# Shifted exp readings as packed 64-bit additions on GpSimd, offset added by VectorE, normalisation moved to VectorE

## The chip, the core and the metric

One core of a Trainium2 chip runs the whole program. Its engines are TensorE (PE, with PEld its weight loads), VectorE (DVE), ScalarE (ACT), GpSimd (POOL) and SyncE (SP), which here only issues DMAs. The metric is the device time of one execution in microseconds; the median over the runs counts. The profile is one execution taken by the hardware profiler; its span runs from the program's first instruction to its last.

## The reference

The reference takes a 2048 x 640 input in bf16, normalises each row, and adds three things: the input, an attention block and a feed-forward block, both on the normalised rows.

```python
def _A_ref(x, wq, wk, wv, wo):            # H = 32 heads, Dh = 20, S = 2048
    q = (x @ wq).reshape(B, S, H, Dh).transpose(0, 2, 1, 3)
    k = x @ wk                            # one k and one v for all heads
    v = x @ wv
    scores = jnp.einsum("bhqd,bkd->bhqk", q, k) * (Dh ** -0.5)
    p = softmax(scores, axis=-1)
    o = jnp.einsum("bhqk,bkd->bhqd", p, v)
    return o.transpose(0, 2, 1, 3).reshape(B, S, H * Dh) @ wo
def _B_ref(x, w1, w2):                    # F = 1728
    return silu(x @ w1) @ w2
xn = layernorm(x)
return x + _A_ref(xn, ...) + _B_ref(xn, ...)
```

There is no mask. The largest part is the exponential: 32 heads x 2048 queries x 2048 keys.

## The kernel before

**Blocks.** Scores are made in transposed form: 128 keys on the partitions, 512 queries of one head along the row. One such tile is a block; it fills one bank of PSUM. There are 2048 blocks: 4 chunks of 512 queries, 32 heads, 16 key tiles. Four heads form a group; their 64 blocks are taken key tile by key tile, and 32 groups follow one another. Since a head has 20 channels only, four heads lie side by side in strips of 32 rows, and the score matmuls of three or four blocks run at the same time in four row strips of the array (line L1113). This is a *step* (`do_S`). The product of the exponentials with v (PV, L954) uses four column strips, one per head of the group, so up to four PV matmuls run together; below, such a set is called a *pass*. The other tiled matmuls (q, feed-forward, output projection; L856) also go in passes of four.

**Two ways to the exponential.** Most blocks go to ScalarE: `exp` over two or three PSUM banks at once, written as bf16 (L1147). The others go to VectorE, in integer arithmetic. The score is scaled so that adding an offset and reading the resulting 16-bit integer as the bits of a bf16 number gives a piecewise linear 2^x. One instruction per block (L1162) clamps the value to 0..32512 and writes it as int16 into a buffer `Z`. To smooth the error, each such block is read three times: as it is, with 43 added, and with 86 added to the integers; the three readings are weighted 1, 0.805 and 0.625 through three copies of v, each with a column that sums the denominator. So a block on ScalarE costs one PV matmul and a block on VectorE three. Three blocks of `Z` are collected, then `flush_z` makes the two shifted readings `Y`: the second shift (86) always on GpSimd (L1199), an int32 addition that treats two 16-bit numbers as one with a tile of the constant 65537 x shift as second input; the first shift (43) on VectorE (L1193, in its fast mode on SBUF data) or on GpSimd, whichever the planner's balance prefers. `Z` has four sets, `Y` one for each.

**The offset.** It enters before through the score matmul itself: rows of q that are otherwise padding hold the offset's two parts (`offq`, 16000 and 45), and a second copy of kT has ones in those rows. Blocks for VectorE use the second copy (`kT[:, 1]`), blocks for ScalarE the first. GpSimd makes the second copy (L1801) and, in the prologue, the offset columns and the tile `qo` from which the q buffer's padding is filled by DMA.

**End of a group.** The accumulated U (numerators and denominators) is copied from PSUM by VectorE (L1243), transposed by a DMA from SP, the reciprocals of the denominators are made on VectorE (L1227), and the product, the normalisation, is made on GpSimd (L1232), for the last group on VectorE. When a chunk's eight groups are done, SP transposes `o`, and the output projection follows. The attention's part is needed doubled, because the feed-forward carries a factor 2 and the end multiplies by 0.5; before, GpSimd doubles wo in place (L1761).

**What sets the order.** The kernel is written as operations with dependencies. A planner in the file (`Sched`, `Builder.step`) runs at build time: it gives each operation an assumed duration, simulates the five queues, and commits operations to each engine in the order that comes out. That order is then fixed in the program, and each engine works through its own queue in order, with semaphore waits between the engines. How many blocks VectorE gets, when PV runs, and where q, feed-forward and projection matmuls are put between the steps, is all decided there, by some 26 parameters that change every 32 blocks (the table `SEG`). `lock` marks GpSimd and VectorE operations that the planner keeps from overlapping. The order of each queue therefore changes as a whole when durations or parameters change.

**Libraries.** GpSimd's affine select (L1576), which makes the identity matrix, is preceded by an instruction that asks for code library 0.

Of the kernel before, what the change touches and what calls it, by code (L numbers as in the profile page):

```python
# [10 lines left out]
I16 = mybir.dt.int16  # L11
# [32 lines left out]
OFF_HI = 16000.0  # L44
OFF_LO = 45.0
# [57 lines left out]
YP_FIX = 0.15  # L103
YP_BLK = 0.426
# [81 lines left out]
class Op:  # L186
# [3 lines left out]
    def __init__(self, eng, dur, fn, deps, prio=0.0, name="", on_sched=None, mode=None):  # L190
# [21 lines left out]
        self.late = 0.0  # L212


LAT = {"pe": 0.222, "act": 0.238, "dve": 0.14, "pool": 0.19, "sp": 0.0}
INF = float("inf")


class Sched:
# [59 lines left out]
    def ready(self, op, extra=0.0):  # L279
        r = 0.0  # L280
        for d in op.deps:
# [9 lines left out]
            if a > r:  # L291
                r = a
# [181 lines left out]
class Builder:  # L474
# [748 lines left out]
    def normalise(self, g, ut, key, eng):  # L1223
# [11 lines left out]
        if eng == "pool":  # L1235
            op.lock = True
# [662 lines left out]
```

## Time and profile before

| | |
|---|---|
| time, median of 3 runs | 677.72 us (676.57 to 678.05) |
| profiled execution, span | 674.7 us; the timed runs lie 1.9 to 3.4 us above it |
| PE busy | 664.7 us, 99% |
| ACT busy | 664.3 us, 98% |
| DVE busy | 618.6 us, 92% |
| POOL busy | 558.5 us, 83% |
| mean granted TensorE clock | 1.00 in every stage |

No time beside the span is given for the profiled execution itself. Busy means that an instruction of the engine is in flight; TensorE's matmuls overlap each other and their ends are modelled, so its share tells only that it is never left alone. A group row reads: line, engine, operation, written and read tiles with shapes, count, then total busy time, mean ns of one, and idle time of the engine just before, with what ended it. Instructions on ScalarE, VectorE and GpSimd overlap a little, so a mean is longer than the distance from one to the next.

### The profile page before, as it was taken

How to read it: one execution, taken by the hardware profiler on the slowest of the kernel's cores; microseconds unless marked ns; L12 is line 12 of the kernel's file. 1: busy time of each engine (PE TensorE's matmuls, PEld its weight loads, DVE VectorE, ACT ScalarE, POOL GpSimd, SP SyncE). 2: the span in 40 equal slices, each digit the busy share in tenths (PEclk: the TensorE clock that was granted, in tenths of full speed). 3: DMA queues.
4: the chain of work that ended last, by engine and by line, in shares of the span. 5: the costliest groups of instructions: out<-in, count | busy, mean ns of one | idle time of the engine just before them, and what ended most of it. 6: DMA issues, size and time to landing. Idle time of an engine off the chain costs nothing.

```text
span 674.7 us, 22669 instructions
## 1 busy us (share of the span) xinstructions
PE 664.7 (99%) x9656; PEld 218.6 (32%) x9656; DVE 618.6 (92%) x1110; ACT 664.3 (98%) x743; POOL 558.5 (83%) x442
## 2 busy tenths in 40 slices
PE   8899999999999999999999999999999999999997
PEld 4332223333323223333323322333332332233333
DVE  7899999899999999989999999999899999999996
ACT  8999999999999999999999999999999999999995
POOL 3385889978978889997988899978989989979983
PEclk9999999999999999999999999999999999999999
DMA  7567100000014000000003210000100310001001
GB/s 208 99 235 238 46 10 8 10 18 15 14 38 106 17 10 11 10 11 18 18 9 50 57 48 10 17 2 13 25 9 19 88 51 5 18 11 28 16 9 41
DMA packets 52729, 28.05 MB, mean 42 GB/s; under 512 B 38582, under 2 KB 51990, under 8 KB 52630
## 3 DMA queue, kind: packets, MB, share of 16 engines
q1 hardware_dynamic: 51174, 26.38, 14.9%
q8 instruction: 78, 1.28, 0.8%
q10 hardware_dynamic: 1456, 0.22, 0.2%
q14 instruction: 21, 0.17, 0.1%
HBM read 11.44 MB, written 2.62 MB: 21 GB/s over the span
## 4 chain that ended last, share of the span: by engine, by line
ACT 54%; PE 41%; DVE 2%; DMA 1%; issue 0%; POOL 0%; SPq 0%
ACT sbt L1147 51%; PE psall L954 14%; PE psall L1113 13%; PE psall L856 13%; ACT sbt L1337 2%; DVE sbt L1162 1%; DMA sbt<-sbt 1%; DMA sbt<-in_A_x_dram 1%; ACT sbt L1661 0%; DVE sbt L1641 0%; POOL sbt L1199 0%; PE psall L1772 0%; DVE sbt L1193 0%; PE psall L1791 0%; DVE sbt L1243 0%
## 5 line engine op out<-in xcount | busy, mean ns | idle before, releaser
L1147 ACT ACTIVATE sbt<-psall 128x1024 bf16<-128x1024 f32 (+1 forms) x649 | 635.5, 1217 | 0.3
L1199 POOL TENSOR_TENSOR sbt<-sbt 128x768 int32<-128x768 int32 x368 | 520.5, 1443 | 79.5 <-DVE sbt L1193 54.4
L1162 DVE TENSOR_SCALAR sbt<-psall 128x512 int16<-128x512 f32 x695 | 456.6, 684 | 40.5 <-PE psall L1113 30.1
L954 PE MATMUL psall<-sbt 128*32 128x512 bf16 x3438 | 260.4, 383 | 0.1
L1113 PE MATMUL psall<-sbt 32*128 32x512 bf16 x2048 | 251.3, 384 | 3.5 <-ACT sbt L1147 1.4
L856 PE MATMUL psall<-sbt 128*32 128x320 bf16 (+2 forms) x3923 | 227.7, 331 | 0.7 <-DVE sbt L1799 0.4
L1113 PEld LDWEIGHTS psall<-sbt 32*128 32x128 bf16 x2048 | 63.1, 91 | 251.3 <-ACT sbt L1147 184.1
L856 PEld LDWEIGHTS psall<-sbt 128*32 128x32 bf16 x3923 | 81.5, 95 | 88.7 <-issue 57.8
L954 PEld LDWEIGHTS psall<-sbt 128*32 128x32 bf16 x3438 | 64.2, 95 | 96.0 <-issue 65.2
L1193 DVE TENSOR_SCALAR sbt<-sbt 128x1536 int16<-128x1536 int16 (+2 forms) x108 | 62.8, 594 | 0.1
L1337 ACT ACTIVATE sbt<-psall 128x512 bf16<-128x512 f32 x54 | 41.6, 770 | 0.0
L1342 DVE SCALAR_TENSOR_TENSOR sbt<-sbt,psall 128x512 bf16<-128x512 bf16 x54 | 36.8, 682 | 2.3 <-ACT sbt L1337 1.2
L1232 POOL TENSOR_TENSOR sbt<-sbt 128x320 bf16<-128x320 bf16 x31 | 22.6, 728 | 6.4 <-DVE sbt L1193 4.2
L1243 DVE CAST sbt<-psall 128x512 bf16<-128x512 f32 x32 | 21.9, 684 | 1.2 <-PE psall L954 0.9
L1801 POOL TENSOR_SCALAR sbt<-sbt 128x256 bf16<-128x256 bf16 x8 | 3.8, 480 | 19.7 <-DVE sbt L1799 13.5
L832 PE MATMUL psall<-sbt 128*128 128x512 bf16 (+4 forms) x50 | 14.2, 427 | 1.3 <-DVE sbt L1580 1.2
L1425 DVE SCALAR_TENSOR_TENSOR sbt<-psall,sbt 128x320 bf16<-128x320 f32 x28 | 13.2, 482 | 1.2 <-PE psall L856 1.1
L1406 DVE SCALAR_TENSOR_TENSOR sbt<-psall,sbt 128x320 bf16<-128x320 f32 x28 | 13.6, 485 | 0.2 <-PE psall L856 0.2
L1294 DVE TENSOR_SCALAR sbt<-psall 128x512 bf16<-128x512 f32 (+1 forms) x19 | 12.9, 678 | 0.1
L1641 DVE BATCH_NORM_STATS2 sbt<-sbt 128x6 f32<-128x320 bf16 x20 | 9.0, 469 | 3.1 <-DMA sbt<-in_A_x_dram 3.1
L1227 DVE RECIPROCAL sbt<-sbt 128x16 f32<-128x16 bf16 x31 | 7.6, 244 | 0.2 <-DMA sbt<-sbt 0.2
L832 PEld LDWEIGHTS psall<-sbt 128*128 128x128 bf16 x50 | 5.0, 109 | 7.9 <-issue 3.7
(68 smaller groups left out, 87.0 us busy)
## 6 DMA issues: line engine op xcount, KB each, us to landing
sbt<-in_A_x_dram SPq DMA_DIRECT2D x32, 160.0 KB, 3.2
out_dram<-sbt SPq DMA_DIRECT2D x15, 160.0 KB, 1.8
sbt<-in_B_w_dram SPq DMA_DIRECT2D x5, 432.0 KB, 5.4
sbt<-sbt SPq DMA_DIRECT2D x105, 20.0 KB
sbt<-in_B_w_dram SPq DMA_DIRECT2D x13, 160.0 KB, 2.9
sbt<-sbt SPq DMA_DIRECT2D x1, 1024.0 KB, 5.7
sbt<-sbt SPq DMA_TRANSPOSE x58, 2.4
sbt<-in_A_wo_dram SPq DMA_DIRECT2D x5, 160.0 KB, 2.7
```

Of the source, the lines that this page charges most:

```text
L832: return pe.matmul(self.bk(b, 0, n), self.zero[:, 0:P], self.zero[:, 0:n], start=True, stop=True)
L856: ins = pe.matmul(self.bk(b, 0, n, r, r + SLOT), w[:, r:r + SLOT], x, start=start, stop=stop, tile_position=(0, r), skip_group_check=True)
L954: ins = pe.matmul(self.bk(ub[k], 0, QW, r, r + SLOT), self.v[:, it.w, it.kt, :], it.x(), start=f, stop=False, tile_position=(0, r), skip_g ...
L1113: ins = pe.matmul(self.bk(bank[x]), self.kT[r:r + SLOT, kk, kt * P:(kt + 1) * P], self.qT[r:r + SLOT, g % 8, (g // 8) % 2, :], start=True, ...
L1147: return a.activation(self.E[:, b0 * QW:(b0 + na) * QW].rearrange("p (b n) -> p b n", n=QW), src, AF.Exp, scale=ACT_SCALE)
L1162: return v.tensor_scalar(self.Z[:, zs, zp * QW:(zp + 1) * QW], self.bk(bb), 0.0, ZMAX, ALU.max, ALU.min)
L1193: sc.new("dve", td, lambda v, k=k: v.tensor_scalar(self.Y[:, zs, k, 0:w], self.Z[:, zs, 0:w], float(PH[k + 1][0]), None, ALU.add), zk, yk, ...
L1199: sc.new("pool", tp, lambda v, k=k, cb=cb: v.tensor_tensor(self.Y[:, zs, k, 0:w].bitcast(I32), self.Z[:, zs, 0:w].bitcast(I32), cb, ALU.ad ...
L1232: op = sc.new(eng, 0.69 if eng == "pool" else t_dve_ps(16 * DH), lambda v: v.tensor_tensor(dst, ut[:, :, :, 0:DH], rb, ALU.mult), [key, (" ...
L1243: sc.new("dve", t_dve_ps(QW), lambda v: v.tensor_copy(self.U[:, up, :], self.bk(ub)), [("B", ub)], [("U", up)], prio=U_PRIO, name=f"Uev{g}")
L1337: sc.new("act", t_act(QW), lambda a: a.activation(t, src, AF.Tanh, scale=0.5), [("B", b)], [("tb", tp)], prio=TH_PRIO, name=f"th{c}_{fk}") ...
L1342: sc.new("dve", t_dve_ps(QW), lambda v: v.scalar_tensor_tensor(out=self.hT[0:rows, fk, :], in0=t, scalar=1.0, in1=src, op0=ALU.add, op1=AL ...
```

## The change

1. Both shifted readings are made on GpSimd, each by one `int64_add` per flush: four 16-bit numbers at once, the shift as an immediate (shift x 0x0001000100010001). The planner reckons 0.18 + 0.218 us per block for one (before 0.15 + 0.426), and the lock between GpSimd and VectorE is no longer set for them. VectorE makes no shifted reading any more.
2. The offset is added by VectorE in the clamp: `max 0, min 32512` becomes `add 16045, min 32512`, and `Z` is unsigned. The second kT copy, the offset rows of q, `offk`, `offq`, `qo` and the constant tile `cy` go; the padding of q is filled with zeros.
3. The normalisation of every group is a VectorE instruction, with the priority that the U copy has.
4. wo is not doubled any more; the denominator column of v is halved instead. The doubled identity `id2` has a tile of its own.
5. GpSimd loads another code library (`all_libraries[1]`) once its prologue work is done; the first `int64_add` waits for it. The planner reckons 8.0 us. The request for library 0 ahead of the affine select (now L1562) stays.
6. The table `SEG` has new rows, and the order of all queues is built anew. Counts in the instruction list, before and after: blocks on VectorE 695 and 713; exp instructions of one, two, three banks 7, 580, 62 and 5, 596, 46; PV matmuls 3438 and 3474 in 880 and 885 passes; steps 643 and 643; readings on GpSimd 368 and 492 instructions; on VectorE 108 and 0; DMAs issued by SP 275 and 275.

The diff, cut to its core:

```diff
-OFF_HI = 16000.0
-OFF_LO = 45.0
+OFF = 16045.0
...
-YP_FIX = 0.15
-YP_BLK = 0.426
+YP_FIX = 0.18
+YP_BLK = 0.218
+LIB = 8.0
...
-        self.kT = sb([P, 2, S], BF16)
+        self.kT = sb([P, S], BF16)
...
-        self.Z = sb([P, NZ, ZB * QW], I16)
-        self.Y = sb([P, NZ, 2, ZB * QW], I16)
+        self.Z = sb([P, NZ, ZB * QW], U16)
+        self.Y = sb([P, NZ, 2, ZB * QW], U16)
...
-                kk = 1 if x in dvs else 0
-                ins = pe.matmul(self.bk(bank[x]), self.kT[r:r + SLOT, kk, kt * P:(kt + 1) * P],
+                ins = pe.matmul(self.bk(bank[x]), self.kT[r:r + SLOT, kt * P:(kt + 1) * P],
...
-                return v.tensor_scalar(self.Z[:, zs, zp * QW:(zp + 1) * QW], self.bk(bb), 0.0, ZMAX,
-                                       ALU.max, ALU.min)
+                return v.tensor_scalar(self.Z[:, zs, zp * QW:(zp + 1) * QW], self.bk(bb), OFF, ZMAX,
+                                       ALU.add, ALU.min)
...
-        for k, e in ((0, y0), (1, "pool")):
-            yk = [("Y", zs, k, i) for i in range(n)]
-            if e == "dve":
-                sc.new("dve", td, lambda v, k=k: v.tensor_scalar(
-                    self.Y[:, zs, k, 0:w], self.Z[:, zs, 0:w], float(PH[k + 1][0]), None, ALU.add), zk, yk,
-                    prio=4.0, name=f"y{k}").lock = True
-                continue
...
-            sc.new("pool", tp, lambda v, k=k, cb=cb: v.tensor_tensor(
-                self.Y[:, zs, k, 0:w].bitcast(I32), self.Z[:, zs, 0:w].bitcast(I32), cb, ALU.add), zk + [("cy",)], yk,
-                prio=4.0, name=f"yp{k}").lock = True
+        for k in range(2):
+            sc.new("pool", YP_FIX + YP_BLK * n, lambda g, k=k: g.int64_add(
+                self.Y[:, zs, k, 0:w].bitcast(I64), self.Z[:, zs, 0:w].bitcast(I64),
+                PH[k + 1][0] * 0x0001000100010001), zk + [("lib",)], [("Y", zs, k, i) for i in range(n)],
+                prio=4.0, name=f"yp{k}")
...
-        op = sc.new(eng, 0.69 if eng == "pool" else t_dve_ps(16 * DH), lambda v: v.tensor_tensor(
+        sc.new("dve", t_dve_ps(16 * DH), lambda v: v.tensor_tensor(
             dst, ut[:, :, :, 0:DH], rb, ALU.mult), [key, ("rL", up)], [("o", h0 + i) for i in range(4)],
-            prio=0.5 if eng == "pool" else -1.0, name=f"nrm{g}")
-        if eng == "pool":
-            op.lock = True
+            prio=U_PRIO if g < self.NG - 1 else -1.0, name=f"nrm{g}")
...
-            pool(0.15, lambda g, k=k: g.memset(self.v[:, k, :, DH:DH + 1], PH[k][1]), [("v0",)],
+            pool(0.15, lambda g, k=k: g.memset(self.v[:, k, :, DH:DH + 1], 0.5 * PH[k][1]), [("v0",)],
...
-            for c in range(DC):
-                pool(0.7, lambda g, c=c: g.tensor_scalar(self.wo[:, c, :], self.wo[:, c, :], 2.0, 1.0, ALU.mult, ALU.mult),
-                     [("wo",)], [("wo",)], prio=2.0)
...
-                sc.new("pool", t_pool(256), lambda g: g.tensor_scalar(d1, dst, self.offk[:, :], 1.0, ALU.add,
-                                                                      ALU.mult), [("kT", j), ("offk",)],
-                       [("kT1", j)], prio=1.0, name=f"k1_{j}").lock = True
...
+        def load_lib(g):
+            g.load_library(library_config.all_libraries[1])
+            return g.memset(self.flag[:, 0:1], 0.0)
+        standard = list(sc.pend["pool"])
+        np_("pool", LIB, load_lib, [], [("lib",)], prio=0.5, name="lib").after = standard
```

More of the change, by code (lines that the diff above doesn't have):

```diff
@@ L6 @@
 import concourse.bass as bass
-from concourse import mybir
+from concourse import library_config, mybir
 BF16 = mybir.dt.bfloat16
 F32 = mybir.dt.float32
-I16 = mybir.dt.int16
+U16 = mybir.dt.uint16
+I64 = mybir.dt.int64
 I32 = mybir.dt.int32
@@ L187 @@
     __slots__ = ("eng", "dur", "fn", "deps", "prio", "seq", "end", "avail", "idx", "inc", "inc_no", "sem",
-                 "on_sched", "name", "dma", "mode", "start", "mm", "work", "then", "lock", "rep", "tile", "kt", "w", "x", "na", "late")
+                 "on_sched", "name", "dma", "mode", "start", "mm", "work", "then", "lock", "rep", "tile", "kt", "w", "x", "na", "late", "after")
     def __init__(self, eng, dur, fn, deps, prio=0.0, name="", on_sched=None, mode=None):
@@ L212, in __init__ @@
         self.late = 0.0
+        self.after = ()
 LAT = {"pe": 0.222, "act": 0.238, "dve": 0.14, "pool": 0.19, "sp": 0.0}
@@ L292, in ready @@
                 r = a
+        for d in op.after:
+            if d.end is None:
+                return INF
+            r = max(r, d.end)
         if op.lock:
@@ L682, in s_reads @@
             c, h = g // 8, 4 * (g % 8) + j
-            k += [("kT1" if x in dvs else "kT", kt // 2), ("kT", kt // 2), ("qb", c % 2, h)] + self.qkeys(c, h)
+            k += [("kT", kt // 2), ("qb", c % 2, h)] + self.qkeys(c, h)
         return k
@@ L995, in pick_dve @@
         got = []
-        cand = [x for x in bs if 4 * x[1] + x[2] < GB - NODB and self.nz[x[0]][x[2]] < int(TILE_CAP * (x[0] + 1)) - int(TILE_CAP * x[0])
-                and self.reads_ready([("kT1", x[1] // 2)]) <= sc.t["pe"] + 1e-9]
+        cand = [x for x in bs if 4 * x[1] + x[2] < GB - NODB and self.nz[x[0]][x[2]] < int(TILE_CAP * (x[0] + 1)) - int(TILE_CAP * x[0])]
         cand.sort(key=lambda x: (self.nz[x[0]][x[2]], -bs.index(x)))
@@ L1118, in do_S @@
         b2 = [x for x in bs if bank[x] == late]
-        op = sc.new("pe", 0.216 + self.switch("S"), lambda pe: mms(pe, b1), self.s_reads(b1, dvs), [("B", bank[x]) for x in b1],
+        op = sc.new("pe", 0.216 + self.switch("S"), lambda pe: mms(pe, b1), self.s_reads(b1), [("B", bank[x]) for x in b1],
                     name=f"S{t}", queue=False)
@@ L1129, in do_S @@
         if b2:
-            o2 = sc.new("pe", 0.0, lambda pe: mms(pe, b2), self.s_reads(b2, dvs), [("B", bank[x]) for x in b2],
+            o2 = sc.new("pe", 0.0, lambda pe: mms(pe, b2), self.s_reads(b2), [("B", bank[x]) for x in b2],
                         name=f"S{t}", queue=False)
@@ L1579, in prologue @@
         pool(0.2, lambda g: g.tensor_copy(self.idb[:, :], self.idf[:, :]), [("idf",)], [("idb",)])
+        pool(0.3, lambda g: g.tensor_scalar(self.id2[:, :], self.idf[:, :], 2.0, 1.0, ALU.mult, ALU.mult), [("idf",)], [("id2",)],
+             prio=0.2)
         np_("dve", 0.3, lambda v: v.memset(self.zero[:, :], 0.0), [], [("zero",)], prio=-1.0, name="zero")
         pool(0.1, lambda g: g.memset(self.eps[:, :], EPS), [], [("eps",)])
-        for k in range(2):
-            pool(0.1, lambda g, k=k: g.memset(self.cy[:, k:k + 1], PH[k + 1][0] * 65537), [], [("cy",)])
         pool(0.7, lambda g: g.memset(self.wk[:, :, :], 0.0), [], [("wk",), ("ost", 2, 0), ("ost", 2, 1)])
```

59 lines of the change are left out of this document (15 added, 44 removed), and 112 rows, old and new, of the table SEG.

## The prediction

> **What bounds the kernel now.** First the page: the engine sums and the costliest groups.
>
> ```profile
> PE 664.7 (99%) x9656; PEld 218.6 (32%) x9656; DVE 618.6 (92%) x1110; ACT 664.3 (98%) x743; POOL 558.5 (83%) x442
> ...
> L1147 ACT ACTIVATE sbt<-psall 128x1024 bf16<-128x1024 f32 (+1 forms) x649 | 635.5, 1217 | 0.3
> L1199 POOL TENSOR_TENSOR sbt<-sbt 128x768 int32<-128x768 int32 x368 | 520.5, 1443 | 79.5 <-DVE sbt L1193 54.4
> L1162 DVE TENSOR_SCALAR sbt<-psall 128x512 int16<-128x512 f32 x695 | 456.6, 684 | 40.5 <-PE psall L1113 30.1
> L1113 PE MATMUL psall<-sbt 32*128 32x512 bf16 x2048 | 251.3, 384 | 3.5 <-ACT sbt L1147 1.4
> L1193 DVE TENSOR_SCALAR sbt<-sbt 128x1536 int16<-128x1536 int16 (+2 forms) x108 | 62.8, 594 | 0.1
> L1232 POOL TENSOR_TENSOR sbt<-sbt 128x320 bf16<-128x320 bf16 x31 | 22.6, 728 | 6.4 <-DVE sbt L1193 4.2
> ```
>
> PE and ACT are both full over the span. Two full engines need a second look: which one has air? The windows by stage come next (columns: PE, PEld, DVE, ACT, POOL busy us), then the order of TensorE's work in one stretch, and one row of the tail.
>
> ```profile
> 20.00:30.00 10.00, 8.10 (x86) 3.69 (x84) 8.74 (x32) 10.00 (x11) 2.52 (x5) 1.00 0.51 114
> 30.00:40.00 10.00, 8.92 (x121) 3.82 (x119) 7.98 (x16) 10.00 (x11) 6.14 (x7) 1.00 0.76 194
> 100.00:150.00 50.00, 50.00 (x774) 16.61 (x767) 46.53 (x78) 50.00 (x55) 43.63 (x34) 1.00 0.05 12
> 600.00:650.00 50.00, 50.00 (x786) 16.87 (x787) 46.81 (x82) 50.00 (x55) 43.69 (x34) 1.00 0.07 16
> ```
> ```profile
> 300.49 0.39 PE L1113 MATMUL psall<-sbt 32*128 32x512 bf16 x3
> 300.81 0.61 PE L954 MATMUL psall<-sbt 128*32 128x512 bf16 x8
> 301.36 0.39 PE L1113 MATMUL psall<-sbt 32*128 32x512 bf16 x3
> 301.68 0.83 PE L954 MATMUL psall<-sbt 128*32 128x512 bf16 x12
> 302.45 0.40 PE L1113 MATMUL psall<-sbt 32*128 32x512 bf16 x4
> ...
> 668.71 2.49 PE L856 MATMUL psall<-sbt 128*32 128x320 bf16 x68
> ```
>
> L1113 is the score step. With eight PV matmuls behind it the next step starts after 0.87 us (300.49 to 301.36), with twelve after 1.09 (301.36 to 302.45). So four matmuls side by side, one pass, cost 0.22, and a step itself 0.43, the changes of tile shape to and fro included. The 68 matmuls of 320 columns are 17 passes in 2.49 us, 0.146 each. The instruction list has 643 steps, 880 PV passes, 369 other passes of 512 columns and 612 of 320: 276 + 194 + 81 + 89 = 640 us of TensorE work that nothing shortens, besides the prologue's matmuls and its fillers. Until 40 us TensorE has air (8.10 and 8.92 of 10) while ACT has none: the start is ACT's. After that neither has any that shows in a window, and the two run in lockstep. I read TensorE as the firmer bound from 40 us on, because step follows step at the price just found, and all idle time ahead of its 2048 score matmuls (the L1113 row) is 3.5 us.
>
> **The change part by part.**
>
> *Blocks and passes.* The new order gives 713 instead of 695 of the 2048 exp blocks to VectorE. ACT loses 18 blocks of 635.5/1353 = 0.470 us: 8.5 us less. But each VectorE block is read three times, so PV matmuls go from 3438 to 3474, and passes from 880 to 885 (a few go with fewer than four): +1.1 us. Steps stay 643; runs between step and other work fall by 5 of some 1253 changes; half of 0.43 - 0.22 each is -0.5. The other passes stay. TensorE: **+0.6 us**, and that counts; ACT's 8.5 us are freed beside an engine that isn't freed.
>
> *VectorE.* Off: 62.8 us of y0. On: 18 blocks of 456.6/695 = 0.66, 11.8 us, and 31 normalisations. The last one ran on VectorE already:
>
> ```profile
> 667.84 0.49 DVE L1232 TENSOR_TENSOR sbt<-psall,sbt 128x320 bf16<-128x320 f32 x1
> ```
>
> 31 x 0.49 = 15.2. Sum 618.6 - 62.8 + 11.8 + 15.2 = 583 us: 86% instead of 92%. Adding the offset in the clamp costs nothing: the same instruction with the same shape, two operations before and after. This hides under TensorE; without that cover it would be a gain.
>
> *GpSimd.* The two-input adds go (520.5), the L1232 group too (22.6); 492 packed additions come (454 of three blocks, 26 of two, 12 of one). The trace has none, so bounds:
>
> ```profile
> L1667 POOL TENSOR_SCALAR sbt<-sbt 128x640 bf16<-128x640 bf16 x3 | 2.6, 874 | 0.0
> L1801 POOL TENSOR_SCALAR sbt<-sbt 128x256 bf16<-128x256 bf16 x8 | 3.8, 480 | 19.7 <-DVE sbt L1799 13.5 <-DVE sbt L1672 5.6 <-DVE sbt L1193 0.5
> ```
>
> One-input work costs 0.22 us + 1.03 ns per element by these two rows. Three blocks are 384 words of 64 bits: 0.62 us if a word is an element, 1.01 if each half is; above stands the two-input add, 1.44. I take 1.01: 454 x 1.01 + 26 x 0.75 + 12 x 0.48 = 484 us of the some 630 between first and last flush (33.5 and 663.5, next rows), 77%, hidden. Both readings of a flush are ready after 2.0 us, against y0 after 0.6 and y1 after 1.5 before; the PV queue is ordered for it. Taken 0; if a reading comes late, the PV behind it waits in order, and with it the next step.
>
> *The second library.* These additions need another code library, loaded after GpSimd's prologue work.
>
> ```profile
> 18.52 2.59 POOL L1667 TENSOR_SCALAR sbt<-sbt 128x640 bf16<-128x640 bf16 x3
> ...
> 33.47 1.47 POOL L1199 TENSOR_TENSOR sbt<-sbt 128x768 int32<-128x768 int32 x1 [2.32 <-DVE sbt L1162]
> ...
> 663.52 1.47 POOL L1199 TENSOR_TENSOR sbt<-sbt 128x768 int32<-128x768 int32 x1 [0.50 <-DVE sbt L1193]
> ```
>
> GpSimd is free from 21.1 to 33.5, when the first flush comes; the new order has the same prologue up to there. A load shorter than 12.4 us is hidden; beyond that it costs one for one.
>
> *The first library.* Both kernels call for library 0 ahead of the affine select (L1576 before, L1562 after). Before, nothing else was ever loaded:
>
> ```profile
> L1576 POOLq MODIFY_POOL_CONFIG  x2: 11/11/11, 1.1 to 1.1; - x2
> ...
> 1.18 0.29 POOL L1576 TENSOR_SCALAR_AFFINE_SELECT sbt<-sbt 128x128 f32<-128x128 f32 x1 [0.17 <-POOL sbt L1583]
> 1.42 0.10 POOL L1583 MEMSET sbt<- 128x1 int32 x1
> ...
> 2.26 0.30 POOL L1588 MEMSET sbt<- 128x240 bf16 x1
> ...
> 5.91 0.54 ACT L1615 ACTIVATE sbt<-sbt 128x400 bf16<-128x400 bf16 x1 [0.73 <-DMA sbt<-in_A_wq_dram]
> ```
>
> The call took 0.02 us and the affine select started at once. The changed kernel ends with the other library loaded, so each further execution should load library 0 anew at 1.1 us, in front of GpSimd's queue. Behind it stand the affine select (0.24 to the next start), the L1588 memset (L1574 after; 0.30), then the identity, the memsets of v and the rest. ACT's copy of wq (L1615) overwrites that memset and waits for it. The load's price is bounded by 0.02 below and above by the largest group of loads:
>
> ```profile
> 35.23 3.51 SPq L1557 DMA_DIRECT2D sbt<-in_B_w_dram  x5
> ...
> sbt<-in_B_w_dram SPq DMA_DIRECT2D x5, 432.0 KB, 5.4
> sbt<-sbt SPq DMA_DIRECT2D x1, 1024.0 KB, 5.7
> ```
>
> Five of 432 KB: 3.5 + 5.4 = 8.9 us. Nearest is a single large transfer, 5.7. Then the memset ends at 1.18 + 5.7 + 0.24 + 0.30 = 7.4, ACT starts at 7.5 instead of 5.91: **+1.6 us**. ACT works nearly without idle from there to the first exp and on to 40 us, so its delay moves the point where TensorE fills up, and the end. At 0.02: no cost; at 8.9: +4.8. The identity, done by 8.3, is still ahead of the first transposes:
>
> ```profile
> 10.19 0.81 PE L1772 MATMUL psall<-sbt 128*128 128x128 bf16 x10 [0.73 <-DVE sbt L1672]
> ```
>
> [...] No row here shows a load, and 0.02 us agrees only with a library that is already there.
>
> *Offsets out of q and k.* GpSimd loses its offset chain and eight kT copies (3.8 us, L1801), five wo doublings and the offset tile. Score matmuls keep their shape. The prologue's first exps are the same list; no blocks come earlier: 0.
>
> *Normalisation on VectorE beside GpSimd.* Behind each one in VectorE's queue wait the clamps that free PSUM banks for the next step, and SP's transposes of o wait for it as they did for GpSimd's (SP issues 275 DMAs in both lists). How VectorE meets GpSimd, the trace shows at the tail and in sum:
>
> ```profile
> 661.73 1.72 DVE L1193 TENSOR_SCALAR sbt<-sbt 128x1536 int16<-128x1536 int16 x1
> ...
> L1193 DVE TENSOR_SCALAR sbt<-sbt 128x1536 int16<-128x1536 int16 x93 | 57.1, 623 | 0.1
> L1193 DVE TENSOR_SCALAR sbt<-sbt x108: 280/550/1715, 38.3 to 663.8; 128x1536 int16<-128x1536 int16 x93, 128x1024 int16<-128x1024 int16 x12, 128x512 int16<-128x512 int16 x3
> ...
> PEld psall L954 <- DVE sbt L1193: 1.5, 7, 0.2
> ```
>
> A y0 with a median of 0.55 took 1.72 beside a running GpSimd add. The 93 large ones lost some 93 x (0.623 - 0.550) = 6.8 us so, and PV waited 1.5 us for them, which goes. The new normalisations may wait the same way: 31 x 0.77 x half of 1.01 = 12 us of VectorE's time, and at 1.5 to 6.8 TensorE sees 2.7 of it. Against that go the 1.5 and the 1.4 us that steps waited for ACT (the L1113 row), which now has less to do. Taken **0**; ends -3 (both go, nothing comes; no more idle than 3.5 us is there) and +12. [...]
>
> Sum: 674.7 + 0.6 + 1.6 + 0 = 676.9 us of span. The median of the runs before is 677.72, 3.0 above the profiled span; 676.9 + 3.0 = **679.9 us**.
>
> **Rivals.** A: the reload is free, as at 1.1 us before; TensorE's +0.6 alone remains: 678.3. For it: 0.02 us; against it: there the library was never exchanged. B, the other side: no reload, and ACT with 8.5 us and VectorE with 36 us less to do stop holding TensorE up; 3 us of air go: 677.7 + 0.6 - 3 = 675.3. It decides once the reload is under 5.91 - 1.18 - 0.24 - 0.30 = 4.2 us, which ACT's wait for wq covers. C: GpSimd becomes the bound, from 630/(454 + 26 x 0.74 + 12 x 0.48) = 1.31 us per addition; at 1.44 it ends 479 x 1.44 - 630 = 60 us later, about 738. D: the second load takes over 12.4 us, or each normalisation's wait reaches TensorE: +3 to +12, 681 to 690.
>
> **How the numbers follow.** Forecast 0.52, A 0.24, B 0.14, C 0.03, D 0.07. A measurement here tells about 0.2%, 1.4 us, from no change. Of the forecast 0.42 is slower than that, 0.09 same, 0.01 faster; of A 0.04, 0.15 and 0.05; B is faster, C and D slower: faster 0.20, same 0.24, slower 0.56. The forecast's own range is 678 to 683. The range for all is 675.0 to 685.0: B below, an 8.9 us reload (683.1) and some waiting above.
>
> **What would show it.** A gap of several us ahead of the affine select, ACT's wq copy near 7.5 us and the first exp near 18.3 instead of 16.69; windows from 100 to 650 with TensorE at 50 of 50, VectorE near 43, GpSimd near 38; additions at 0.6 to 1.0 us start to start. Wrong, if the affine select starts at 1.2, if TensorE shows windows with air, or if GpSimd is full.

## The result and the profile after

The changed kernel takes 678.96 us (median of 17 runs, 677.41 to 681.58), the kernel before beside it 676.72 (17 runs, 676.14 to 679.2): a ratio of 1.0026, 95% interval 1.0015 to 1.0037. In a later repeat, 12 runs gave 678.21 against 677.96, 0.9998 (0.9984 to 1.0012). So the change is worth nothing, or costs up to 0.4%. The profiled execution has a span of 677.4 us, 2.7 above the one before.

Its page: the engine sums, the chain that ended last by engine, and the groups that answer to those shown of before.

```profile
PE 663.8 (98%) x9694; PEld 219.6 (32%) x9694; DVE 596.3 (88%) x1051; ACT 658.0 (97%) x741; POOL 401.9 (59%) x514
...
PE 50%; ACT 43%; DVE 5%; issue 2%; POOL 0%; POOLq 0%; ACTq 0%
...
L1149 ACT ACTIVATE sbt<-psall 128x1024 bf16<-128x1024 f32 (+1 forms) x647 | 628.6, 1150 | 2.9 <-PE psall L1115 2.2
L1188 POOL INT64_ADD sbt<-sbt x492 | 393.5, 813 | 238.8 <-DVE sbt L1164 233.3
L1164 DVE TENSOR_SCALAR sbt<-psall 128x512 uint16<-128x512 f32 x713 | 465.8, 685 | 54.8 <-PE psall L1115 45.8
...
L1115 PE MATMUL psall<-sbt 32*128 32x512 bf16 x2048 | 251.1, 384 | 4.3 <-ACT sbt L1149 2.5
```

GpSimd's busy time fell from 558.5 to 401.9 us, VectorE's from 618.6 to 596.3 and ScalarE's from 664.3 to 658.0, as meant. The span did not follow. Where the time is, the start shows. First GpSimd, up to the first additions (start, duration, operation, and in brackets the idle time ahead of it):

```profile
0.91 0.63 POOL L1570 MEMSET sbt<- 128x640 bf16 x1
9.77 0.28 POOL L1562 TENSOR_SCALAR_AFFINE_SELECT sbt<-sbt 128x128 f32<-128x128 f32 x1 [8.23 <-issue]
10.02 0.29 POOL L1574 MEMSET sbt<- 128x240 bf16 x1
...
23.30 2.58 POOL L1640 TENSOR_SCALAR sbt<-sbt 128x640 bf16<-128x640 bf16 x3 [9.31 <-DVE sbt L1645]
32.13 0.09 POOL L1792 MEMSET sbt<- 128x1 f32 x1 [6.24 <-issue]
38.69 1.63 POOL L1188 INT64_ADD sbt<-sbt  x2 [6.47 <-DVE sbt L1164]
```

A library load has no row of its own here: the call's two rows (L1562) are of 11 ns each, as they were before, and the load is idle time that ends with "issue". There are two. The reload of library 0 ahead of the affine select is 8.23 us, where before the affine select started at 1.18. The load of the second library, at 26 us, is 6.24 us, and after it GpSimd still waits 6.47 us for its first `Z`: that load is hidden. Behind the first stands ScalarE:

```profile
4.98 0.19 ACT L1602 ACTIVATION_READ_ACCUMULATOR sbt<-sbt 128x1 f32 x1
10.40 0.54 ACT L1588 ACTIVATE sbt<-sbt 128x400 bf16<-128x400 bf16 x1 [5.23 <-POOL sbt L1574]
```

Its copy of wq waits for the memset L1574 behind the affine select and starts at 10.40 instead of 5.91. TensorE waits in turn. Its order of work in the same place, before and after (L1772 and L1738 are transposes, L1791 and L1757 the k projection, L832 and L836 fillers, L1113 and L1115 the first score step):

```profile
10.84 1.00 PE L832 MATMUL psall<-sbt 128*128 128x512 bf16 x4
11.95 0.71 PE L1791 MATMUL psall<-sbt 128*128 128x256 bf16 x5
...
14.81 0.73 PE L856 MATMUL psall<-sbt 128*32 128x256 bf16 x20
...
16.12 0.60 PE L1113 MATMUL psall<-sbt 32*128 32x512 bf16 x6
```
```profile
11.33 1.00 PE L836 MATMUL psall<-sbt 128*128 128x512 bf16 x4
15.74 0.74 PE L1757 MATMUL psall<-sbt 128*128 128x256 bf16 x5 [3.41 <-ACT sbt L1746]
...
17.48 1.26 PE L860 MATMUL psall<-sbt 128*32 128x256 bf16 x20
...
20.11 0.73 PE L860 MATMUL psall<-sbt 128*32 128x256 bf16 x20
...
21.34 0.60 PE L1115 MATMUL psall<-sbt 32*128 32x512 bf16 x6
```

The k projection is 3.8 us late (15.74 against 11.95), after 3.41 us of idle time. Then the same work takes longer: from its start to the second set of 20 matmuls 4.37 us against 2.86, and one set of 20 took 1.26 us where the later one took 0.73. The windows of one microsecond say why (columns as in the prediction; the one behind the busy times is the granted clock):

```profile
15.00:16.00 1.00, 0.26 (x3) 0.24 (x4) 0.34 (x1) 1.00 (x4) 0.00 (x0) 1.00 0.00 0
16.00:17.00 1.00, 1.00 (x12) 0.97 (x10) 0.48 (x3) 0.97 (x3) 0.00 (x0) 0.66 0.00 0
17.00:18.00 1.00, 1.00 (x18) 0.69 (x19) 0.83 (x4) 1.00 (x4) 0.00 (x0) 0.50 0.00 0
18.00:19.00 1.00, 1.00 (x17) 0.33 (x10) 1.00 (x5) 0.78 (x3) 0.00 (x0) 0.50 0.00 0
```

After the gap TensorE was granted half its clock for some 3.4 us, which costs 1.5 here. So the start is 5.2 us late: 3.8 for the late library and 1.5 for the clock. Yet the span grew by 2.7 only. The rest of the new order must be about 2.5 us faster than the old one.

### The profile page after: what moved, and what is told of

The parts are those of the page before. It is cut to its first block, busy times and chain, and to the rows that moved or that the text cites. A ratio compares the mean times of both kernels' runs of the same rounds, so it can differ in the third digit from the quotient of the medians.

```text
span 677.4 us, 22745 instructions
## 1 busy us (share of the span) xinstructions
PE 663.8 (98%) x9694; PEld 219.6 (32%) x9694; DVE 596.3 (88%) x1051; ACT 658.0 (97%) x741; POOL 401.9 (59%) x514
## 4 chain that ended last, share of the span: by engine, by line
PE 50%; ACT 43%; DVE 5%; issue 2%; POOL 0%; POOLq 0%; ACTq 0%
ACT sbt L1149 40%; PE psall L958 18%; PE psall L1115 16%; PE psall L860 15%; DVE sbt L1164 3%; ACT sbt L1323 2%; DVE sbt L1411 1%; DVE sbt L1222 1%; ACT sbt L1599 0%; ACT sbt L1634 0%; PE psall L1757 0%; PE psall L1313 0%; DVE sbt L1328 0%; DVE sbt L1231 0%; ACT sbt L1602 0%
## 5 line engine op out<-in xcount | busy, mean ns | idle before, releaser
L1149 ACT ACTIVATE sbt<-psall 128x1024 bf16<-128x1024 f32 (+1 forms) x647 | 628.6, 1150 | 2.9 <-PE psall L1115 2.2
L1188 POOL INT64_ADD sbt<-sbt x492 | 393.5, 813 | 238.8 <-DVE sbt L1164 233.3
L1164 DVE TENSOR_SCALAR sbt<-psall 128x512 uint16<-128x512 f32 x713 | 465.8, 685 | 54.8 <-PE psall L1115 45.8
L958 PE MATMUL psall<-sbt 128*32 128x512 bf16 x3474 | 264.0, 383 | 0.1
L1115 PE MATMUL psall<-sbt 32*128 32x512 bf16 x2048 | 251.1, 384 | 4.3 <-ACT sbt L1149 2.5
L860 PE MATMUL psall<-sbt 128*32 128x320 bf16 (+2 forms) x3923 | 224.9, 332 | 0.1
L1115 PEld LDWEIGHTS psall<-sbt 32*128 32x128 bf16 x2048 | 62.8, 91 | 249.9 <-ACT sbt L1149 183.1
L1222 DVE TENSOR_TENSOR sbt<-sbt 128x320 bf16<-128x320 bf16 x31 | 18.9, 611 | 0.3
L836 PE MATMUL psall<-sbt 128*128 128x512 bf16 (+3 forms) x52 | 14.9, 432 | 1.2 <-DVE sbt L1568 1.2
L1757 PE MATMUL psall<-sbt 128*128 128x256 bf16 x40 | 6.4, 284 | 3.4 <-ACT sbt L1746 3.4
L1640 POOL TENSOR_SCALAR sbt<-sbt 128x640 bf16<-128x640 bf16 x3 | 2.6, 874 | 9.3 <-DVE sbt L1645 9.3
L836 PEld LDWEIGHTS psall<-sbt 128*128 128x128 bf16 x52 | 5.3, 110 | 8.5 <-issue 4.5
```

Of the source, the lines that this page charges most:

```text
L836: return pe.matmul(self.bk(b, 0, n), self.zero[:, 0:P], self.zero[:, 0:n], start=True, stop=True)
L860: ins = pe.matmul(self.bk(b, 0, n, r, r + SLOT), w[:, r:r + SLOT], x, start=start, stop=stop, tile_position=(0, r), skip_group_check=True)
L958: ins = pe.matmul(self.bk(ub[k], 0, QW, r, r + SLOT), self.v[:, it.w, it.kt, :], it.x(), start=f, stop=False, tile_position=(0, r), skip_g ...
L1115: ins = pe.matmul(self.bk(bank[x]), self.kT[r:r + SLOT, kt * P:(kt + 1) * P], self.qT[r:r + SLOT, g % 8, (g // 8) % 2, :], start=True, sto ...
L1149: return a.activation(self.E[:, b0 * QW:(b0 + na) * QW].rearrange("p (b n) -> p b n", n=QW), src, AF.Exp, scale=ACT_SCALE)
L1164: return v.tensor_scalar(self.Z[:, zs, zp * QW:(zp + 1) * QW], self.bk(bb), OFF, ZMAX, ALU.add, ALU.min)
```

## The experiments

Theory 1: the two halves just named. What the start loses passes to the end one for one, and without it the new order is faster than the kernel before. Theory 2, nearer to the prediction: the body gains nothing, since TensorE is the firmer bound, and the 5.2 us are partly taken up again later, so that 2.7 remain.

**The library restored at the end.** After GpSimd's last instruction the changed kernel loads library 0 again, so that the next execution finds it.

```diff
                 for fn in lists["pool"]:
                     fn(e)
+                e.load_library(library_config.all_libraries[0])
+                e.memset(b.flag[:, 1:2], 0.0)
```

> The changed kernel with one addition: after its last packed addition GpSimd loads library 0 again, so that the next execution finds it in place. All queues are else the same. Theory 1 (the reload at the start costs its whole 5.2 us, and the rest of the new order is 2.5 us faster than the old): the affine select starts near 1.8 us, the first score matmul at 16.1 instead of 21.3, the span falls from 677.4 to 672.2, and the ratio to the kernel before is 0.996. Theory 2 (the new order gives nothing, a late start is half made up for by slack behind it): the start is the same as in theory 1, but the span is 674.7 and the ratio 1.000. Either way the load at the end, 6 to 8 us from 660 on, is hidden behind the last projections, or else the end moves by up to 1 us.

674.15 us, ratio 0.994 (0.9917 to 0.9962), span 672.1; repeated later on the same chip 673.92, 0.9943 (0.9924 to 0.9962), span 672.2. No other kernel here that does all of the work is as fast. GpSimd's timeline at both ends:

```profile
1.81 0.29 POOL L1562 TENSOR_SCALAR_AFFINE_SELECT sbt<-sbt 128x128 f32<-128x128 f32 x1 [0.29 <-POOL sbt L1570]
...
657.42 2.37 POOL L1188 INT64_ADD sbt<-sbt  x4 [0.41 <-DVE sbt L1164]
667.36 0.09 POOL L1819 MEMSET sbt<- 128x1 f32 x1 [7.56 <-issue]
```

The affine select starts at once again, and the load at the end, 7.56 us, ends 4.7 us ahead of the last instruction: it lies beside the output projection. Matched exp by exp, the changed kernel runs 5.17 us behind this one (the repeat's trace) from the first exp to the last, without a change in between: a rigid shift, none of it taken up again. Theory 1 holds.

**The swap alone, in the kernel before.** The other library is loaded at the end of the kernel before, which uses nothing of it; the queues are else the same.

```diff
                 for fn in lists["pool"]:
                     fn(e)
+                e.load_library(library_config.all_libraries[1])
+                e.memset(b.flag[:, 0:1], 0.0)
```

> The kernel before with one addition: after its last addition GpSimd loads the other library, which nothing uses, so that the next execution must load library 0 at its start. Queues else the same. Theory 1 (a late start passes one for one): first score matmul near 21.3 instead of 16.1, span 674.7 + 5.2 = 679.9, ratio 1.0077. Theory 2 (half of it is absorbed): same start, span 677.4, ratio 1.004.

684.0 us, ratio 1.0084 (1.0061 to 1.0107), span 682.3: more than either theory's figure. GpSimd, then ScalarE:

```profile
9.61 0.28 POOL L1577 TENSOR_SCALAR_AFFINE_SELECT sbt<-sbt 128x128 f32<-128x128 f32 x1 [8.63 <-issue]
9.86 0.09 POOL L1584 MEMSET sbt<- 128x1 int32 x1
9.89 0.62 POOL L1585 MEMSET sbt<- 128x640 bf16 x1
```
```profile
10.61 0.54 ACT L1613 ACTIVATE sbt<-sbt 128x400 bf16<-128x400 bf16 x1 [6.60 <-POOL sbt L1585]
11.05 0.72 ACT L1630 ACTIVATE sbt<-sbt 128x640 bf16<-128x640 bf16 x1
```

In this order the memset of wk too stands behind the reload, and ScalarE's copy of wk, which goes first, waits from about 4 us on. The first exp is 7.4 us late, and every later one up to 618 us between 7.36 and 7.40. Of this 6.7 us are the lateness of ScalarE's copy (10.61 instead of 3.94); TensorE was at half clock here too, from 13.5 to 20.4 us, and what that adds was not parted from the rest. In both kernels the price of the reload is thus set mainly by how long ScalarE, the first engine behind it, can work without it (it waits 5.23 us in the changed kernel and 6.60 here), and it is paid in full (5.17 us and 7.4).

**The half clock.** The restoring kernel's traces show a clock of 1.00 at the start. To part the two costs of the reload in the changed kernel, TensorE got filler work, 15 more matmuls, in the gap of 3.41 us.

```diff
+            more = 15 if self.nfill == 28 else 0
             def fn(pe):
+                for _ in range(more):
+                    pe.matmul(self.bk(b, 0, n), self.zero[:, 0:P], self.zero[:, 0:n], start=True, stop=True)
                 return pe.matmul(self.bk(b, 0, n), self.zero[:, 0:P], self.zero[:, 0:n], start=True, stop=True)
```

> The changed kernel (span 677.4), with one of TensorE's filler matmuls of the start made 15 times more (512 columns, zeros, into a bank that holds nothing): 15 x 0.22 = 3.2 us of work in the place where TensorE stands idle for 3.41 us, ahead of the 128x256 matmuls at 15.74 us, while ScalarE's late copies are awaited. Nothing else is changed, and nothing left out. In the changed kernel that idle time is followed by a granted clock of 0.50 from 16.3 to 19.6 us, and the work from 15.74 to 20.11 takes 4.37 us against 2.86 before. Theory H (the late library has two costs: 3.8 us of lateness, and 1.5 us because the idle TensorE is then granted half its clock): clock 1.00 in these windows, the first score step at 19.8 instead of 21.34, span 675.9. Rival (the half clock comes of itself, or of something else at the start): clock 0.50 again, 677.4.

> The changed kernel once more, on the same chip as the one with the filled gap, to be compared with it: 677.4 us of span, half clock from 16 to 20 us, and a median 1.5 us above the other's by theory H; the two alike by the rival.

Neither came out. With the fillers 679.77 us (1.0023, 1.0002 to 1.0045), without them 678.21 (0.9998, given above). TensorE's timelines, first with the fillers, then the repeat of the changed kernel without:

```profile
11.43 1.23 PE L1742 MATMUL psall<-sbt 128*128 128x128 bf16 x10 [3.12 <-POOL sbt L1569]
...
13.31 3.84 PE L839 MATMUL psall<-sbt 128*128 128x512 bf16 x14
...
17.39 0.71 PE L1761 MATMUL psall<-sbt 128*128 128x256 bf16 x5
...
21.43 0.60 PE L1119 MATMUL psall<-sbt 32*128 32x512 bf16 x6
```
```profile
12.58 0.80 PE L1738 MATMUL psall<-sbt 128*128 128x128 bf16 x10 [2.99 <-DVE sbt L1645]
13.22 1.72 PE L836 MATMUL psall<-sbt 128*128 128x512 bf16 x4
15.29 1.25 PE L1757 MATMUL psall<-sbt 128*128 128x256 bf16 x5 [0.35 <-ACT sbt L1746]
...
20.03 0.60 PE L1115 MATMUL psall<-sbt 32*128 32x512 bf16 x6
```

The reload opens an earlier gap as well: the first transposes wait 3.12 us for the identity (L1569). With this one the half clock came, from 10.8 to 14.2 us; the first of the added matmuls ran under it, and the k projection, which stands behind them in TensorE's queue, started at 17.39 only, 1.0 us after ScalarE's copy was done. A second stretch of half clock at 38 us, in no trace of the changed kernel itself, added 1.3 to a span of 678.8. In the repeat the same gap, 2.99 us here, brought the half clock from 13.4 to 16.8 us, most of it in time in which TensorE would have waited for ScalarE anyway: the first step came at 20.03, 3.9 us later than in the restoring kernel, and the span was 676.1. So the half clock follows the reload's gaps, but where it falls, and what it costs, changes from run to run. From the k projection to the first step TensorE took 4.7 us in the repeat, 5.6 in the first profile and 4.1 in the restoring kernel: the half clock cost 0.6 and 1.5. In the runs of the changed kernel the mean granted clock was below 0.999 in 27 of 29, in those of the restoring kernel in 1 of 14, and in the runs of the kernel before beside all these variants in 26 of 64. So with the reload the half clock came nearly always here, but it came without it too. With the fillers it was 7 of 12, so they did keep it away in some runs; but the spans of the other five, 676.0 to 677.1, are no shorter than those of the repeat (675.3 to 677.4), as the fillers take time themselves. That the clock costs 1.5 us whenever the library is reloaded is not shown.

**The first shifted reading off VectorE.** In the kernel before, VectorE's y0 writes 8 columns instead of up to 1536, once each buffer has been written in full; PV then reads old values. In the trace of before such a reading of 128x1536 in SBUF takes a mean of 0.62 us (L1193), a clamp of 128x512 out of PSUM 0.68 (L1162).

```diff
+                wx = w if self.full_y[zs] < w else 8
+                self.full_y[zs] = max(self.full_y[zs], w)
...
-                    self.Y[:, zs, k, 0:w], self.Z[:, zs, 0:w], float(PH[k + 1][0]), None, ALU.add), zk, yk,
+                    self.Y[:, zs, k, 0:wx], self.Z[:, zs, 0:wx], float(PH[k + 1][0]), None, ALU.add), zk, yk,
```

> The kernel before, all queues in the same order, but the first shifted reading, where VectorE makes it, is written in full only until each buffer set was filled once; after that VectorE writes 8 columns instead of up to 1536 and PV reads old values (work left out: most of 108 shifted readings). Theory A (the shifted readings on VectorE, and their waits for GpSimd, held TensorE up): 1.5 to 3 us less, ratio 0.996 to 0.998. Theory B (full ACT held it up): no change, ratio 0.999 to 1.001.

676.45 us against 677.58, ratio 0.9981 (0.9963 to 0.9999), span 674.4. VectorE's 31 us less gave 0.3 in the span, and matched exp by exp this gain is there at 100 us and does not grow after. The medians differ by more, 1.1 us, but the kernel before was below a mean clock of 0.999 in 9 of 19 runs and this one in 4 of 12; among the other runs the gap is 0.8. That y0 on VectorE held TensorE up through the body, for 1.5 to 3 us (theory A), is not seen; a share of under 1 us is not excluded.

**Less work for ScalarE, before the change.** 18 exps of two banks make one bank; the other bank's exponentials are left out.

```diff
+            self.n_two += na == 2
+            nx = 1 if na == 2 and self.n_two > 60 and self.n_two % 28 == 0 else na
...
-            def efn(a, run=run, na=na, b0=b0, step=step):
+            def efn(a, run=run[:nx], na=nx, b0=b0, step=step):
```

> The kernel before, all queues in the same order, but 18 of the two-bank exps, spread over the body, make only one of their two banks (work left out: 18 blocks' exponentials; PV reads old values). ACT has 18 x 0.43 = 7.7 us less to do, about what the change takes from it. Theory A (VectorE's shifted readings held TensorE up): no change, ratio 0.999 to 1.001. Theory B (full ACT held TensorE up): 2 to 3 us less, ratio 0.996 to 0.997.

674.14 us, ratio 0.9939 (0.9916 to 0.9961), span 672.4: of some 7.7 us of ScalarE's time, 2.3 reach the span, growing evenly from 200 us on. So the full ScalarE did hold TensorE up (theory B), and the 8.5 us that the change takes from it are enough for the gain of 2.5 in the body. That nothing else in the new order adds to the gain is not shown by this.

**The same in the restoring kernel, and the opposite.** The edit just shown in the restoring kernel, where it halves 19 exps (some 8.1 us), and in another variant 14 additional exps of 128x512 from a tile of zeros.

```diff
+            self.n_two += na == 2
+            again = na == 2 and self.n_two > 40 and self.n_two % 39 == 0
...
             def efn(a, run=run, na=na, b0=b0, step=step, again=again):
+                if again:
+                    a.activation(self.spare[:, :], self.zero[:, :], AF.Exp, scale=ACT_SCALE)
```

> The kernel that restores the library at its end (span 672.1), with ACT's relief taken back: in 14 places spread over the run ScalarE makes one more exponential of one bank's width, 128x512, from a tile of zeros into a spare tile that nobody reads. It comes right ahead of a two-bank exp, after that one's wait. 14 x about 0.55 = 7.7 us of ScalarE's time come back; all queues are else the same, and nothing is left out. Theory B (the body's gain is ScalarE's relief, of which some 0.3 reaches the time, 2.3 of 7.7 us in the run that took ScalarE work away): span near 674.4, growing steadily over the body. Rival 1 (the body's gain has to do with VectorE and GpSimd, ScalarE is off the path): 672.1 to 672.5. Rival 2 (ScalarE is now the bound alone): one for one, 679.8.

> The kernel that restores the library at its end (span 672.1), with still less for ScalarE: some 18 of its two-bank exps, spread evenly from the 84th on, make only their first bank (part of the exponentials is left out: stale values are read in their place), about 7.7 us of ScalarE's time; all queues are else the same. If ScalarE still holds TensorE up as it did before the change (2.3 of 7.7 us): span near 669.8. If the new order has used that up and TensorE alone bounds (own estimate of TensorE's idle time from 40 us on is about 1 us here, 3 us before): 671 to 672.1.

> The kernel that restores the library at its end, once more, beside the two variants on the same chip: 672.1 us of span and a ratio of 0.994 to the kernel before, if the gain is a thing of the kernel and not of the chip that it ran on.

Less: 673.05 us (0.9931, 0.9911 to 0.9952), span 671.2, a gain of 1.0 of 8.1, the smaller of the two figures expected. More: 681.58 us (1.0057, 1.0036 to 1.0077), span 679.0, 6.8 above the 672.2 of the repeat. ScalarE's timeline shows an added exp; 0.52 us later the next starts:

```profile
113.85 0.72 ACT L1154 ACTIVATE sbt<-sbt 128x512 bf16<-128x512 bf16 x1
114.37 26.43 ACT L1156 ACTIVATE sbt<-psall 128x1024 bf16<-128x1024 f32 x28
```

14 x 0.52 = 7.3 us cost 6.8. Of the three cases expected, the one-for-one price came nearest, and the 2.3 was wrong: here a price found by taking work away (2.3 of 7.7) did not hold for adding it (6.8 of 7.3).

**More work, in both kernels and on both engines.** The same additional exps in the kernel before; and every 45th score step made three times into the same banks, in the kernel before and in the restoring one.

```diff
+        extra = 2 if self.nv % 45 == 44 else 0
+        def mms1(pe):
+            for _ in range(extra):
+                mms(pe, b1)
+            return mms(pe, b1)
-        op = sc.new("pe", 0.216 + self.switch("S"), lambda pe: mms(pe, b1),
+        op = sc.new("pe", 0.216 + self.switch("S"), mms1,
```

> The kernel before (span 674.7 us), with 14 more ScalarE exponentials of 128x512 from a tile of zeros into a spare tile, each right ahead of a two-bank exp, spread over the run as in the same edit of the restoring kernel, where each took 0.52 us of ScalarE's queue, 7.3 us in all, and the span grew by 6.8 us. Nothing is left out. Theory C (in both orders TensorE and ScalarE stand in lockstep: more on either costs nearly all of it, less on one gives little): +6 to +7.3, span near 681. Theory P (the prediction's reading: before the change TensorE was the firmer bound and ScalarE's time lay beside it): 0 to +2.5, span at most 677.

> The kernel before, where every 45th score step is made three times into the same banks (14 steps, 28 more passes of TensorE at the 0.22 us of the timeline = 6.2 us); nothing is left out, and all queues are else the same. Theory P and theory C both expect nearly all of it: +5 to +6.2, span 680 to 681. If ScalarE were the bound alone: 0 to +2.

> The same edit, every 45th score step made three times, in the kernel that restores the library at its end (span 672.1). Theory C: +5 to +6.2, span 677 to 678.3, as in the kernel before. If the new order has made ScalarE the bound alone, as the 6.8 us for 7.3 us of more ScalarE work could also be read: 0 to +2, at most 674.

More ScalarE in the kernel before: 683.37 us (1.0086, 1.0072 to 1.0099), span 681.6. This kernel has fewer two-bank exps, and 13 were added (L1152 x13), 6.8 us; the span grew by 6.9. More TensorE: 682.52 us in the kernel before (1.0067, 1.0046 to 1.0089), span 681.2; 679.83 in the restoring one (1.0036, 1.0022 to 1.005), span 679.3. A step made three times delays the next work by 0.76 us (114.82 to 115.58 below) where a single one takes 0.33 (113.84 to 114.17), so 14 of them are some 6.0 us. Both profiles also hold a stretch at half clock in the prologue, ahead of the first repeated step (67 us), in the kernel before along with a DMA that came 1.8 us late; they must be read without it. Kernel before, timeline of one repeated step and windows:

```profile
113.84 0.39 PE L1113 MATMUL psall<-sbt 32*128 32x512 bf16 x3
114.17 0.73 PE L856 MATMUL psall<-sbt 128*32 128x320 bf16 x16
114.82 0.82 PE L1113 MATMUL psall<-sbt 32*128 32x512 bf16 x9
115.58 0.59 PE L856 MATMUL psall<-sbt 128*32 128x320 bf16 x12
```
```profile
30.00:40.00 10.00, 8.40 (x88) 3.38 (x88) 5.41 (x13) 8.01 (x9) 3.86 (x5) 0.83 0.78 183
100.00:150.00 50.00, 50.00 (x756) 16.28 (x753) 45.99 (x78) 49.83 (x55) 43.88 (x33) 1.00 0.05 12
```

Matched exp by exp, the kernel before with more TensorE work is 3.3 us late at 66 us and 6.9 at the end, so the body cost 3.6. The restoring kernel is 1.4 late at 66 us and 6.8 at the end: 5.4. The runs with a mean clock of 0.999 or more agree: spans of 678.3 and 678.6 us against 674.8 to 676.0 for the kernel before beside them, and 677.3 to 678.4 for the restoring kernel. The 3.6 lies between the two figures expected. What one engine's change in work gives in the span of the profiled executions:

| | kernel before | restoring kernel |
|---|---|---|
| ScalarE less | -2.3 of 7.7 us | -1.0 of 8.1 us |
| ScalarE more | +6.9 of 6.8 us | +6.8 of 7.3 us |
| TensorE more | +3.6 of some 6 us | +5.4 of some 6 us |

By the medians the first row is -3.4 and -0.9 us, the second +6.3 and +7.7; part of the difference is runs at half clock. Theory P (TensorE the firmer bound before the change) falls at the second row: added ScalarE work cost all of it. Theory C, lockstep, is the reading that fits, with ScalarE the firmer one before the change and both about equally firm after it.

## Why the prediction was right, and where

The forecast of 679.9 is 0.9 us above the measured median, and the sign came out in the first set of runs; in the repeat no change was seen. The 0.9 is about what the median of the kernel before moved, from 677.72 to 676.72: as a change, 2.2 us were forecast and 2.2 measured. But two terms of the sum were off by more than 3 us each, in opposite directions, so that it came out is luck.

*First library (+1.6; measured 3.8, and 5.2 with the clock).* The mechanism was right in each link: the reload, the affine select, the memset behind it, ScalarE's copy of wq, then TensorE. The size of the reload was not: 8.23 us against the 5.7 taken from one large transfer; the upper bound of 8.9 held. The lower one, the call's 0.02 us, told nothing of a load: the call's rows are the same here, with the load behind them. The copy started at 10.40 instead of 7.5, the first exp at 22.3 instead of 18.3. The load of the other library, at 26 us, took 6.24, 2.0 us less. And the step had no term for the half clock that came behind TensorE's idle time: 1.5 us in the profiled run, 0.6 in the repeat. In four traces it lasted some 3.4 us; the gaps that it came with were 3.41 (changed kernel), 2.99 (its repeat), 3.12 (fillers) and 1.96 us (last section). With the swap it lasted 6.9, and the gap was 5.92. A gap of 1.41 us in the changed kernel, ahead of its first transposes, left the clock full, and so did one of 0.96 (last section).

*Blocks and passes (+0.6), and "ACT's 8.5 us are freed beside an engine that isn't freed".* This step failed. The body became about 2.5 us faster. ScalarE was the firmer bound, and two rows that the prediction quotes said so: ahead of its exps ScalarE had been idle for 0.3 us in the whole run, TensorE ahead of its score matmuls for 3.5. The chain that ended last, of the kernel before, has the same:

```profile
ACT 54%; PE 41%; DVE 2%; DMA 1%; issue 0%; POOL 0%; SPq 0%
```

With more ScalarE work in the kernel before, and with less, the same line reads:

```profile
ACT 85%; PE 12%; DVE 1%; DMA 1%; SPq 0%; issue 0%; POOL 0%
PE 86%; ACT 8%; DVE 3%; DMA 1%; issue 1%; SPq 0%; POOL 0%
```

So a near-even split goes with lockstep here, and the greater part lay with ScalarE. The windows could not tell: 50.00 of 50 for both. That ScalarE's relief is enough for the gain is shown by the run that took such work from the kernel before (2.3 for 7.7 us; by this rate 8.5 us give 2.5). That it is the whole cause is argued: how the planner's other differences add to it was not tried.

*VectorE (583 us; measured 596.3)* was summed from group rows, whose instructions overlap, so that taking a group away frees less than its row: in the kernel before all durations add up to 682.9 us, where VectorE is busy for 618.6. The share of 88% instead of 86% matters little: the run with the small y0 took more than that from VectorE and gained 0.3 us of span.

*GpSimd (1.01 us an addition; measured 0.80 from start to start)*: a pair takes 1.63 (38.69 above), a single one 0.82. The price lay between the bounds, the additions take 393.5 us instead of the 484 reckoned, and TensorE's idle time ahead of the steps went from 3.5 to only 4.3. Hidden, as predicted.

*The second library (hidden below 12.4 us)*: right, 6.24.

*Normalisation (12 us of VectorE's time, 0 in the sum)*: the wait is real but smaller. The line's summary in the trace (minimum, median and longest in ns), then VectorE and GpSimd in one place:

```profile
L1222 DVE TENSOR_TENSOR sbt<-sbt x31: 475/483/1074, 59.6 to 660.3; 128x320 bf16<-128x320 bf16 x31
```
```profile
322.18 1.07 DVE L1222 TENSOR_TENSOR sbt<-sbt 128x320 bf16<-128x320 bf16 x1
```
```profile
322.08 1.85 POOL L1188 INT64_ADD sbt<-sbt  x2 [1.05 <-DVE sbt L1164]
```

A normalisation that starts while an addition runs takes up to 1.07 us instead of 0.48. Their mean is 0.611 (31 take 18.9 us together), so VectorE lost 31 x 0.13 = 4 us. Before, the same work on GpSimd had a mean of 0.73. Of the 31, 16 start while an addition runs and take 0.48 to 1.07 us; the other 15 take 0.47 or 0.48. A part of the wait does reach the time: of the long ones four, 0.87 to 1.07 us each, stand in the chain that ended last, each with clamps queued behind it, in this trace and in both of the restoring kernel. The one above, there:

```profile
322.18 1.07 DVE sbt L1222
```

At 0.48 us these four would be some 2 us shorter. That is an estimate of the most that their waits cost; TensorE's own idle time until a clamp was done is 0.6 us in the whole run, and what the waits really cost was not tried.

*Offsets out of q and k (0)* were not tried alone.

*The rivals.* A (the reload is free) and C (GpSimd bound) are out by the rows above. Of D the second load is hidden, and the normalisations' waits are smaller than the 3 to 12 us that it asks for. B is the telling one: its first half, that there is no reload, is false, but its second, that a relieved ScalarE lets TensorE run 3 us faster, is what happened, and where the reload was taken out its sum (675.3 as a time) came within 1.2 us of the 674.15 measured.

## What to carry to other kernels

The library that this program leaves loaded is a cost at the start of its next execution: 8.23 us on GpSimd, 5.2 of span. If a kernel changes GpSimd's library, try restoring the first one in the tail, where GpSimd is idle (here the load ended 4.7 us ahead of the end), and measure the steady state. Where two engines are both full, read which of them never waits (the idle time ahead of its main group, and the chain's shares) before calling one the bound, and test it by adding a known piece of work to each; taking work away gave a much smaller answer here (1.0 of 8.1 us, against 6.8 of 7.3, in the restoring kernel) and told only how near the second engine is. The delay ahead of this body in lockstep was paid in full (5.17 us from the first exp to the last), so here a hidden microsecond at the start was worth as much as one in the loop.

## What was unexpected

The load of a library is not one number. Two things differ between the loads, and the traces part them somewhat. The first is which library it is: library 0 took 7.78 to 8.89 us at the start (four traces) and 6.85 to 7.56 at the end (five), the other one 6.06 to 6.83 in the middle (eight) and 5.84 at the end (one). At the end, with the DMA engines at 0.02 of their time or less, library 0 is thus more than 1 us longer. The second is the place: at the start, with the DMA engines at 0.9 or more, the same library takes about 1 us longer than at the end. That it is the transfers that make it longer was not tried.

The half clock does not need the reload. In the restoring kernel with more TensorE work a gap of 1.96 us in the prologue, ahead of the first transposes, was enough in one run (timeline, then window):

```profile
10.36 0.88 PE L1744 MATMUL psall<-sbt 128*128 128x128 bf16 x10 [1.96 <-DVE sbt L1651]
```
```profile
12.00:13.00 1.00, 1.00 (x5) 0.43 (x4) 1.00 (x5) 0.97 (x4) 0.00 (x0) 0.50 1.07 376
```

It cost 1.4 us at the first exp. The fillers ahead of this gap (L836) ended at 8.40 us in this run and at 9.36 in the repeat of the restoring kernel, where the gap was 0.96 and the clock stayed full. Part of the scatter between executions, which reaches 5 us in the kernel before, probably comes from such stretches: in the batch of 19 runs the three slowest (681.3 to 681.5) are those with the lowest mean clock, 0.995.
